# Attention over a K/V cache with two MLP branches: reading K, V and the left-over weight rows in longer elements that feed several partitions

## The chip, the cores and the metric

One core of a Trainium2 chip. The metric is the device time of one execution in microseconds; 214.95 us is the median of three runs of the kernel before (214.92 to 214.96). Engines: PE does matmuls (PEld loads their weights), DVE, ACT and POOL do elementwise work, SP issues nearly all transfers. Sixteen DMA engines move the data.

## The reference

Four sequences (B = 4) with one new token of width 576 each. `out = x + A(LN(x)) + M(LN(x))`.

- A is attention: `q = LN(x) @ wq` gives 32 heads of 128; the cache holds 16 K and V heads, each used by two q heads, of which the last 2,048 positions count; then softmax, the product with V and `@ wo`.
- M normalizes again, goes through `w1` and a gelu, shifts four quarters of the columns along the sequence (with one token all of them become zero), `@ w2`, adds; then a layer norm, `w3` to width 4,608, gelu, `w4`, adds.

Nearly everything that is read is read once: K and V are 16 heads x 2 MB each (67.1 MB), the weights 21.4 MB.

## The kernel before

All is bf16 in memory. A unit of work is one K or V head *g* for all four sequences: 4 x 2,048 positions x 128, a tile of [128 partitions x 8,192 elements], 2 MB. The 2,048 positions are cut into 32 pieces *i* of 64 consecutive positions, and partition `4 i + b` holds piece *i* of sequence *b*: 16,384 B in a row (`kv_pairs`, L231). The K ring has four slots and the V ring four (`NKS`, `NVS`).

Weights of 576 rows are laid out as 4 x 128 rows ("main", four consecutive rows a partition) and 64 left-over rows ("rag"). A left-over row is halved over two partitions, so these 64 rows also fill 128 partitions (`rag_src`, L183). Such rests exist for wq, w1, w2 and w3, of 4,096, 576, 576 and 4,608 B a partition.

Every instruction is put in a list for its engine with a key, and the lists are sorted by key (L563), so the order of the work is fixed by hand. `add_dma` (L172) puts a transfer in SP's list; each transfer has 16 counts on its semaphore. SP issues in this order: wq, w1, w2, w3; the K tiles 0 to 8, V tile 0, K tiles 9 to 15; V tiles 1 to 3; wo into K slots; V tiles 4 to 15; w4 in five pieces. From K tile 4 on, SP waits for PE to be through with the tile four before (`T..`); V likewise (`PV..`); wo waits for K tile 14.

PE's work, in the same order:

- the front: transposes of the normalized x, q (L301), the two small products of M, and w3 (L515);
- K: each tile is transposed in 64 matmuls (L337) with `perm_k` as the moving operand. `perm_k` is a permutation that also sorts the columns from `(i b)` to `(b i)`, so that sequence *b* finds its positions side by side (`kttile`, L76). DVE and ACT copy the results out of PSUM (L344, L345); the scores are 16 matmuls a tile (L353);
- the softmax: exponentials by ACT (L384), 32 x 32 transposes by DVE (L387) and a matmul with `perm_p` (L388), which puts the probabilities on the partitions that V has. `bmask` (L407) marks which sequence a partition belongs to;
- V: 64 matmuls a tile (L434), then wo (L449, L464), w4 (L449, L531), two copies and the output from two queues (L558).

`perm_k` and `perm_p` are made by POOL (L207, L209) and `bmask` by DVE (L407), all from one identity matrix at the start.

Of the kernel before, what the change touches and what calls it, by code (L numbers as in the profile page):

```python
# [8 lines left out]
ALU = mybir.AluOpType  # L9
AX = mybir.AxisListType  # L10


NKS = 4
NVS = 4
# [24 lines left out]
def bass_parallel_sum__sliding_block_cached__mixer_s_mlp__decode_kernel(  # L39
    nc, A_x, A_k_cache, A_v_cache, A_wq, A_wo, B_x, B_w1, B_w2, B_w3, B_w4, out  # L40
):
    B, Sq, D = A_x.shape
    _, Hkv, Sk, Dh = A_k_cache.shape
    Hq = A_wq.shape[1] // Dh
    F = B_w3.shape[1]
    W = min(4096, max(256, Sk // 4))
    assert (B, D, Hkv, Dh, Hq, W, Hq // Hkv, F) == (4, 576, 16, 128, 32, 2048, 2, 4608)
    G = Hkv
    NT = W // 32
    UE = NT * 128  # L50
# [11 lines left out]
    with ExitStack() as ctx:  # L62
# [7 lines left out]
        vring_t = sb("vring", [128, NVS * UE], BF16)  # L70
# [7 lines left out]
        w3rag = regB_t[:, 4 * F:W3E]  # L78
        wqmain = vring_t[:, 0:4 * Hq * Dh].rearrange("p (r n) -> p r n", r=4)
        wqrag = vring_t[:, 4 * Hq * Dh:4 * Hq * Dh + Hq * Dh // 2]  # L80
        wo_sb = kring_t[:, 0:32 * D].rearrange("p (r n) -> p r n", r=32)
        _o = 4 * Hq * Dh + Hq * Dh // 2
        w1main = vring_t[:, _o:_o + 4 * D].rearrange("p (r n) -> p r n", r=4)
        _o += 4 * D
        w1rag = vring_t[:, _o:_o + HALF]
        _o += HALF
        w2main = vring_t[:, _o:_o + 4 * D].rearrange("p (r n) -> p r n", r=4)
        _o += 4 * D
        w2rag = vring_t[:, _o:_o + HALF]
# [22 lines left out]
        ident_bf = sb("ident_bf", [128, 128], BF16)  # L112
        perm_k = sb("perm_k", [128, 128], BF16)
        perm_p = sb("perm_p", [128, 128], BF16)
        bmask = sb("bmask", [128, B, 2], FP32)
# [42 lines left out]
        S = {}  # L158
# [9 lines left out]
        def add(engine, emit, waits=(), sig=None, key=0.0, loop=None):  # L168
            seqc[0] += 1
            prog[engine].append(Op(emit, waits, sig, key, seqc[0], loop))  # L170

        def add_dma(pairs, skey, waits=(), key=0.0, engine="sp"):  # L172
            if skey not in S:
                S[skey] = sem("s_" + "_".join(str(k) for k in (skey if isinstance(skey, tuple) else (skey,))))
            dma_count[skey] = dma_count.get(skey, 0) + 16 * len(pairs)

            def emit(e):
                for o_, i_ in pairs:
                    e.dma_start(o_, i_).then_inc(S[skey], 16)  # L179
            add(engine, emit, waits, None, key)  # L180
            return ("dma", skey, dma_count[skey])

        def rag_src(w_ap):  # L183
            return w_ap[512:576, :].rearrange("r (h n) -> (r h) n", h=2)

        KS = float(NHB + 4)
        KV = KS + 4.0
# [3 lines left out]
        P = lambda *a, **k: add("pool", *a, **k)  # L191
# [10 lines left out]
        def first_counts(e):  # L202
# [1 line left out]
                e.sem_inc(S[("eb", 32 - NTB + k)], 1)  # L204
                e.sem_inc(S[("on", k)], 1)
        P(first_counts, key=-95.7)
        P(lambda e: e.tensor_copy(out=perm_k[:].rearrange("p (b i) -> p b i", b=B), in_=ident_bf[:].rearrange("p (i b) -> p b i", b=B)),  # L207
          waits=["ident_bf"], sig="perm_k", key=-95.5)
        P(lambda e: e.tensor_copy(out=perm_p[:].rearrange("p (i b) -> p i b", b=B), in_=ident_bf[:].rearrange("p (b i) -> p i b", b=B)),  # L209
          waits=["ident_bf"], sig="perm_p", key=-95)  # L210
        P(lambda e: e.memset(ident_f[:], 1.0), sig="if1", key=-94)
        P(lambda e: e.affine_select(out=ident_f[:], in_=ident_f[:], compare_op=ALU.is_equal, fill=0.0, base=0,
# [6 lines left out]
        ev_wq, ev_w3, ev_k, ev_v, ev_w4 = [], [], [], [], []  # L219
        wq_src = A_wq[0:512, :].rearrange("(p r) n -> p r n", r=4)  # L220
        for r in (0, 2):
            ev_wq += 2 * [add_dma([(wqmain[:, r:r + 2, :], wq_src[:, r:r + 2, :])], ("wq", r), (), -20 + r)]
        ev_wq.append(add_dma([(wqrag, rag_src(A_wq))], ("wq", 4), (), -15))
        ev_w1 = add_dma([(w1main, B_w1[0:512, :].rearrange("(p r) n -> p r n", r=4)), (w1rag, rag_src(B_w1))], "w1", (), -14)
        ev_w2 = add_dma([(w2main, B_w2[0:512, :].rearrange("(p r) n -> p r n", r=4)), (w2rag, rag_src(B_w2))], "w2", (), -13)
        w3_src = B_w3[0:512, :].rearrange("(p r) n -> p r n", r=4)
        for r in (0, 2):
            ev_w3 += 2 * [add_dma([(w3main[:, r:r + 2, :], w3_src[:, r:r + 2, :])], ("w3", r), (), -12 + r)]
        ev_w3.append(add_dma([(w3rag, rag_src(B_w3))], ("w3", 4), (), -8))

        def kv_pairs(ring_t, slot, cache, g):  # L231
            return [(ring_t[:, slot * UE:(slot + 1) * UE],
                     cache[:, g, Sk - W:Sk, :].rearrange("b (i t) d -> i b (t d)", t=NT))]

        for g in range(G):
            ev_k.append(add_dma(kv_pairs(kring_t, g % NKS, A_k_cache, g), ("k", g % NKS),
                                [f"T{8 * (g - NKS) + 7}"] if g >= NKS else [], g))
        wo_wait = f"T{8 * (G - 2) + 7}"
        for g in range(G):
            kk = KS + g if g else V0_AFTER + 0.5  # L240
            w = [f"PV{g - NVS}"] if g >= NVS else (["hs1"] if g < WQ_SLOTS else [])
            ev_v.append(add_dma(kv_pairs(vring_t, g % NVS, A_v_cache, g), ("v", g % NVS), w, kk))
            if g == WO_AFTER:
                ev_wo = add_dma([(kring_t[:, 0:32 * D], A_wo.rearrange("(p r) n -> p (r n)", r=32))],
                                "wo", [wo_wait], kk + 0.1)
# [113 lines left out]
        for n in range(NHB):  # L359
            p = n % 32  # L360
# [3 lines left out]
            eng, f = evac(n)  # L364
# [32 lines left out]
        for g in range(G):  # L397
# [6 lines left out]
        add("dve", lambda e: e.reciprocal(out=rinv[:], in_=rsum[:]), waits=["rsum"], sig="rinv", key=KS + 0.36)  # L404
        add("dve", lambda e: e.tensor_scalar(out=diag[:], in0=ident_f[:], scalar1=rinv[:, 0:1], scalar2=None, op0=ALU.mult),
            waits=["rinv", "ident_f"], sig="diag", key=KS + 0.37)
        add("dve", lambda e: e.tensor_reduce(out=bmask[:, :, 0], in_=ident_bf[:].rearrange("p (i b) -> p b i", b=B), axis=AX.X, op=ALU.add),  # L407
            waits=["ident_bf"], sig="bmask0", key=-41)
        add("dve", lambda e: e.tensor_copy(out=bmask[:, :, 1], in_=bmask[:, :, 0]), waits=["bmask0"], sig="bmask", key=-40.9)
        add("pe", lambda e: e.matmul(rinvps, lhsT=ones_f[:], rhs=diag[:], start=True, stop=True), waits=["diag", "ones_f", "PTs3"],  # L410
# [235 lines left out]
```

## Time and profile before

| | us |
|---|---|
| median of three runs | 214.95 |
| the profiled execution | 215.35 |
| its span, from the first to the last instruction | 214.0 |
| packets of SP's queue | 6,920, 88.50 MB |
| HBM read over the span | 414 GB/s |

The profile is of one execution, so sums over its rows are made against 215.35 and its span. "PE 139.3 (65%)" means that matmuls ran in 139.3 us of the span. In the rows of forty slices each digit is a tenth of busy time in 5.35 us. The chain of waits is followed back from the last instruction, at each step to what released it. In the rows on DMA issues the last column is the median time from issue to landing, which includes the wait behind earlier transfers. The share of a queue is the time that its packets took, of 16 engines; over a short window it can come out over 100%, since a packet is counted whole where it starts.

### The profile page before, as it was taken

To read this page: it belongs to the slowest core of one execution; us is meant where nothing else is said; L and a number is where in the kernel's file an instruction comes from. 1 tells how busy PE (TensorE), PEld (TensorE's weight loads), DVE (VectorE), ACT (ScalarE), POOL (GpSimd) and SP (SyncE) were. 2 spreads that over 40 slices of the span, in tenths; PEclk is the share of its full clock that TensorE was granted. 3 is DMA by queue.
4 is the path that set the end of the run, shared out by engine and by line. 5 is a ranking of instruction groups with operands and counts; after the bars stand their busy time and mean duration, and the time that the engine had idled before them with its cause. 6 is when DMAs were issued, how large, how long until landed. Compare 5 with 4: busy or idle time off the path is not lost.

```text
span 214.0 us, 5789 instructions
## 1 busy us (share of the span) xinstructions
PE 139.3 (65%) x2670; PEld 108.2 (51%) x2672; DVE 85.1 (40%) x162; ACT 59.3 (28%) x72; POOL 10.8 (5%) x38
## 2 busy tenths in 40 slices
PE   0368375999999994999999719913344443333585
PEld 0114222877777883788887604813333443333444
DVE  5502602666666664466666569611111111100000
ACT  2001222466665553265666653000000000000000
POOL 8201000000000000000000000000000000000000
PEclk9999855899999999699999995555555555555579
DMA  7999999999999999999999999999999999999992
GB/s 243 426 398 447 441 405 435 416 424 426 432 423 429 429 432 426 429 429 430 426 429 429 432 429 441 423 423 426 426 432 429 423 429 426 429 432 425 428 408 108
DMA packets 6946, 88.63 MB, mean 414 GB/s; under 512 B 781, under 2 KB 1177, under 8 KB 1945
## 3 DMA queue, kind: packets, MB, share of 16 engines
q1 hardware_dynamic: 6920, 88.50, 97.7%
q8 instruction: 7, 0.11, 0.2%
q14 instruction: 3, 0.02, 0.0%
q10 hardware_dynamic: 16, 0.01, 0.0%
HBM read 88.49 MB, written 0.00 MB: 414 GB/s over the span
## 4 chain that ended last, share of the span: by engine, by line
DMA 52%; PE 36%; DVE 4%; SPq 4%; issue 2%; ACT 0%
DMA vring<-in_A_v_cache_dram 23%; PE ps L337 23%; DMA kring<-in_A_k_cache_dram 21%; DMA vring<-in_B_w_dram 8%; PE ps L353 7%; PE ps L434 4%; SPq L179 4%; PE ps L531 1%; DVE PTb L387 1%; DVE rmax L379 1%; DVE regB L345 1%; DVE PTs L395 1%; PE ps L410 0%; ACT P_sb L384 0%; DVE out_sb L558 0%
## 5 line engine op out<-in xcount | busy, mean ns | idle before, releaser
L345 DVE COPY regB<-ps 128x1024 bf16<-128x1024 bf16 x80 | 52.4, 687 | 34.3 <-PE ps L337 32.5
L337 PEld LDWEIGHTS ps<-perm_k,kring 128*128 128x128 bf16 x1024 | 58.9, 99 | 11.9 <-issue 8.6
L337 PE MATMUL ps<-perm_k,kring 128*128 128x128 bf16 x1024 | 62.2, 222 | 3.5 <-DMA kring<-in_A_k_cache_dram 3.5
L344 ACT ACTIVATE regB<-ps 128x1024 bf16<-128x1024 bf16 x48 | 47.6, 1022 | 41.1 <-PE ps L337 41.1
L434 PE MATMUL ps<-PTg,vring 128*128 128x8 bf16 x1024 | 29.5, 168 | 39.4 <-DMA vring<-in_A_v_cache_dram 37.0
L434 PEld LDWEIGHTS ps<-PTg,vring 128*128 128x128 bf16 x1024 | 28.4, 104 | 40.4 <-DMA vring<-in_A_v_cache_dram 27.5
L442 DVE TENSOR_TENSOR PTb<-ps,PTb 128x32 bf16<-128x32 f32 x16 | 3.1, 191 | 56.5 <-PE ps L434 56.5
L353 PE MATMUL ps<-regB,Qs 128*32 128x512 bf16 x272 | 18.8, 397 | 4.6 <-issue 3.5
L541 ACT ACTIVATE P_sb<-ps 100x288 f32<-100x288 f32 x1 | 0.4, 410 | 75.8 <-PE ps L449 75.8
L353 PEld LDWEIGHTS ps<-regB,Qs 128*32 128x32 bf16 x272 | 6.6, 97 | 10.8 <-issue 6.4
L398 DVE TENSOR_TENSOR PTg<-PTs,bmask 128x512 bf16<-128x512 bf16 x16 | 10.7, 681 | 0.0
L375 POOL COPY Qs<-Qpad 128x128 bf16<-128x128 bf16 x16 | 4.6, 293 | 92.6 <-PE ps L353 81.2
L515 PE MATMUL ps<-regB,x1nT 128*32 128x432 bf16 (+1 forms) x60 | 5.4, 520 | 1.9 <-DMA regB<-in_B_w_dram 1.4
L279 PE MATMUL ps<-ident_bf,xn_bf 4*128 4x4 bf16 x8 | 0.6, 170 | 8.8 <-DVE ragsrc L272 8.8
L301 PE MATMUL ps<-vring,xnT 128*32 128x512 bf16 x40 | 4.6, 629 | 2.1 <-DMA vring<-in_A_wq_dram 2.1
L388 PE MATMUL ps<-PTb,perm_p 128*128 128x512 bf16 x3 | 1.8, 609 | 4.9 <-DVE PTb L387 4.8
L279 PEld LDWEIGHTS ps<-ident_bf,xn_bf 4*128 4x128 bf16 x8 | 0.4, 112 | 8.8 <-POOL ones_f L215 6.3
L528 DVE STREAM_TRANSPOSE h2T_sb<-PTb 128x1152 bf16<-128x1152 bf16 x1 | 1.4, 1378 | 8.3 <-ACT PTb L525 8.3
L515 PEld LDWEIGHTS ps<-regB,x1nT 128*32 128x32 bf16 x60 | 2.0, 132 | 4.8 <-DMA regB<-in_B_w_dram 2.7
L558 DVE CAST out_sb<-ps 36x144 bf16<-36x144 f32 x1 | 0.3, 300 | 9.8 <-PE ps L531 9.8
L449 PE MATMUL ps<-kring,ORT 128*4 128x288 bf16 x64 | 3.8, 429 | 0.4 <-DVE ORT L463 0.4
L265 ACT ACTIVATE sd<-mv 4x1 f32<-4x1 f32 x3 | 0.6, 202 | 12.1 <-DVE mv L263 12.1
(98 smaller groups left out, 72.0 us busy)
## 6 DMA issues: line engine op xcount, KB each, us to landing
kring<-in_A_k_cache_dram SPq DMA_DIRECT2D x16, 2048.0 KB, 15.7
vring<-in_A_v_cache_dram SPq DMA_DIRECT2D x16, 2048.0 KB, 17.6
regB<-in_B_w_dram SPq DMA_DIRECT2D x2, 2304.0 KB, 21.5
kring<-in_A_wo_dram SPq DMA_DIRECT2D x1, 4608.0 KB, 24.0
vring<-in_A_wq_dram SPq DMA_DIRECT2D x2, 2048.0 KB, 9.8
vring<-in_B_w_dram SPq DMA_DIRECT2D x2, 2016.0 KB, 17.5
vring<-in_B_w_dram SPq DMA_DIRECT2D x2, 576.0 KB, 13.8
vring<-in_B_w_dram SPq DMA_DIRECT2D x1, 720.0 KB, 14.3
```

Of the source, the lines that this page charges most:

```text
L179: e.dma_start(o_, i_).then_inc(S[skey], 16)
L301: ins = e.matmul(Qps[32 * j:32 * j + 32, k, :], lhsT=x_, rhs=w, start=(r == 0), stop=(r == 4), tile_position=(0, 32 * j))
L337: ins = e.transpose(tb[n % NTB][:, t, :], kring[:, g % NKS, 8 * k + t, :], perm_k[:])
L344: return "act", lambda e: e.activation(out=ktbuf[:, n % NKT], in_=src, func=ACTF.Copy)
L345: return "dve", lambda e: e.tensor_copy(out=ktbuf[:, n % NKT], in_=src)
L353: ins = e.matmul(Sps[32 * b:32 * b + 32, c4, :].rearrange("p (t i) -> p t i", t=16), lhsT=Qs[:, g % 4, b, :], rhs=kttile[:, t0:t0 + 16, b, :],
L375: P(lambda e, g=g: e.tensor_copy(out=Qs[:, g % 4], in_=Qpad[:, g]), waits=(["qT"] if g == 0 else []) + ([f"SC{g - 4}"] if g >= 3 else []), ...
L398: add("dve", lambda e, g=g: e.tensor_tensor(out=PTg[:, g % NPG], in0=PTs[:, :, 2 * g:2 * g + 2].unsqueeze(2).to_broadcast([128, NT, B, 2]) ...
L434: ins = e.matmul(OTps(g), lhsT=vring[:, g % NVS, t, :], rhs=PTg[:, g % NPG, t].rearrange("p b e -> p (b e)"), start=(t == 0), stop=(t == N ...
L442: add("dve", lambda e, g=g: e.tensor_tensor(out=OTx[:, :, 2 * g:2 * g + 2, :], in0=OTps(g).rearrange("p (b e) -> p b e", b=B).unsqueeze(3) ...
L449: return e.matmul(ACC[h], lhsT=lhsT, rhs=rhs, start=start, stop=stop, tile_position=(k0, 32 * h))
L515: ins = e.matmul(H2ps[k][32 * j:32 * j + 32, :], lhsT=x_, rhs=w, start=(r == 0), stop=(r == 4), tile_position=(0, 32 * j))
```

## The change

K and V: the 2,048 positions are cut into 16 pieces *i* of 128 consecutive positions, 32,768 B each. The source of a transfer has 16 x 4 such elements, the destination has 128 partitions of 16,384 B as before: an element of the source fills two partitions, so that position half *j* of piece *i* of sequence *b* is on partition `8 i + 2 b + j`. A new helper, `copy_folded`, builds this copy directly on SP's queue, since the two sides no longer have elements of one length. `perm_k`, `perm_p` and `bmask` follow the new order.

Left-over rows: the source is now 16 elements of four whole rows each, which fill eight partitions; the partition of each half row stays as it was.

The names and the sizes of the tiles, the semaphores, the waits and the order of all lists stay.

```diff
--- before.py
+++ after.py
@@ -169,19 +169,23 @@
             seqc[0] += 1
             prog[engine].append(Op(emit, waits, sig, key, seqc[0], loop))
 
-        def add_dma(pairs, skey, waits=(), key=0.0, engine="sp"):
+        def copy_folded(e, dst, src):
+            return e.add_instruction(mybir.InstDMACopy(mode="Copy", name=f"I-{nc.next_id()}", engine=e.engine, ins=e.lower_ap_dma(src),
+                                                       outs=e.lower_ap_dma(dst), queue="qSPDynamicHW"))
+
+        def add_dma(pairs, skey, waits=(), key=0.0, engine="sp", folded=()):
             if skey not in S:
                 S[skey] = sem("s_" + "_".join(str(k) for k in (skey if isinstance(skey, tuple) else (skey,))))
             dma_count[skey] = dma_count.get(skey, 0) + 16 * len(pairs)
 
             def emit(e):
-                for o_, i_ in pairs:
-                    e.dma_start(o_, i_).then_inc(S[skey], 16)
+                for n, (o_, i_) in enumerate(pairs):
+                    (copy_folded(e, o_, i_) if n in folded else e.dma_start(o_, i_)).then_inc(S[skey], 16)
             add(engine, emit, waits, None, key)
             return ("dma", skey, dma_count[skey])
 
         def rag_src(w_ap):
-            return w_ap[512:576, :].rearrange("r (h n) -> (r h) n", h=2)
+            return w_ap[512:576, :].rearrange("(e r) n -> e (r n)", e=16)
 
         KS = float(NHB + 4)
         KV = KS + 4.0
@@ -204,9 +208,9 @@
                 e.sem_inc(S[("eb", 32 - NTB + k)], 1)
                 e.sem_inc(S[("on", k)], 1)
         P(first_counts, key=-95.7)
-        P(lambda e: e.tensor_copy(out=perm_k[:].rearrange("p (b i) -> p b i", b=B), in_=ident_bf[:].rearrange("p (i b) -> p b i", b=B)),
+        P(lambda e: e.tensor_copy(out=perm_k[:].rearrange("p (b i j) -> p b i j", b=B, j=2), in_=ident_bf[:].rearrange("p (i b j) -> p b i j", b=B, j=2)),
           waits=["ident_bf"], sig="perm_k", key=-95.5)
-        P(lambda e: e.tensor_copy(out=perm_p[:].rearrange("p (i b) -> p i b", b=B), in_=ident_bf[:].rearrange("p (b i) -> p i b", b=B)),
+        P(lambda e: e.tensor_copy(out=perm_p[:].rearrange("p (i b j) -> p i b j", b=B, j=2), in_=ident_bf[:].rearrange("p (b i j) -> p i b j", b=B, j=2)),
           waits=["ident_bf"], sig="perm_p", key=-95)
         P(lambda e: e.memset(ident_f[:], 1.0), sig="if1", key=-94)
         P(lambda e: e.affine_select(out=ident_f[:], in_=ident_f[:], compare_op=ALU.is_equal, fill=0.0, base=0,
@@ -220,26 +224,26 @@
         wq_src = A_wq[0:512, :].rearrange("(p r) n -> p r n", r=4)
         for r in (0, 2):
             ev_wq += 2 * [add_dma([(wqmain[:, r:r + 2, :], wq_src[:, r:r + 2, :])], ("wq", r), (), -20 + r)]
-        ev_wq.append(add_dma([(wqrag, rag_src(A_wq))], ("wq", 4), (), -15))
-        ev_w1 = add_dma([(w1main, B_w1[0:512, :].rearrange("(p r) n -> p r n", r=4)), (w1rag, rag_src(B_w1))], "w1", (), -14)
-        ev_w2 = add_dma([(w2main, B_w2[0:512, :].rearrange("(p r) n -> p r n", r=4)), (w2rag, rag_src(B_w2))], "w2", (), -13)
+        ev_wq.append(add_dma([(wqrag, rag_src(A_wq))], ("wq", 4), (), -15, folded=(0,)))
+        ev_w1 = add_dma([(w1main, B_w1[0:512, :].rearrange("(p r) n -> p r n", r=4)), (w1rag, rag_src(B_w1))], "w1", (), -14, folded=(1,))
+        ev_w2 = add_dma([(w2main, B_w2[0:512, :].rearrange("(p r) n -> p r n", r=4)), (w2rag, rag_src(B_w2))], "w2", (), -13, folded=(1,))
         w3_src = B_w3[0:512, :].rearrange("(p r) n -> p r n", r=4)
         for r in (0, 2):
             ev_w3 += 2 * [add_dma([(w3main[:, r:r + 2, :], w3_src[:, r:r + 2, :])], ("w3", r), (), -12 + r)]
-        ev_w3.append(add_dma([(w3rag, rag_src(B_w3))], ("w3", 4), (), -8))
+        ev_w3.append(add_dma([(w3rag, rag_src(B_w3))], ("w3", 4), (), -8, folded=(0,)))
 
         def kv_pairs(ring_t, slot, cache, g):
-            return [(ring_t[:, slot * UE:(slot + 1) * UE],
-                     cache[:, g, Sk - W:Sk, :].rearrange("b (i t) d -> i b (t d)", t=NT))]
+            return [(ring_t[:, slot * UE:(slot + 1) * UE].unsqueeze(1),
+                     cache[:, g, Sk - W:Sk, :].rearrange("b (i t) d -> i b (t d)", t=2 * NT))]
 
         for g in range(G):
             ev_k.append(add_dma(kv_pairs(kring_t, g % NKS, A_k_cache, g), ("k", g % NKS),
-                                [f"T{8 * (g - NKS) + 7}"] if g >= NKS else [], g))
+                                [f"T{8 * (g - NKS) + 7}"] if g >= NKS else [], g, folded=(0,)))
         wo_wait = f"T{8 * (G - 2) + 7}"
         for g in range(G):
             kk = KS + g if g else V0_AFTER + 0.5
             w = [f"PV{g - NVS}"] if g >= NVS else (["hs1"] if g < WQ_SLOTS else [])
-            ev_v.append(add_dma(kv_pairs(vring_t, g % NVS, A_v_cache, g), ("v", g % NVS), w, kk))
+            ev_v.append(add_dma(kv_pairs(vring_t, g % NVS, A_v_cache, g), ("v", g % NVS), w, kk, folded=(0,)))
             if g == WO_AFTER:
                 ev_wo = add_dma([(kring_t[:, 0:32 * D], A_wo.rearrange("(p r) n -> p (r n)", r=32))],
                                 "wo", [wo_wait], kk + 0.1)
@@ -404,7 +408,7 @@
         add("dve", lambda e: e.reciprocal(out=rinv[:], in_=rsum[:]), waits=["rsum"], sig="rinv", key=KS + 0.36)
         add("dve", lambda e: e.tensor_scalar(out=diag[:], in0=ident_f[:], scalar1=rinv[:, 0:1], scalar2=None, op0=ALU.mult),
             waits=["rinv", "ident_f"], sig="diag", key=KS + 0.37)
-        add("dve", lambda e: e.tensor_reduce(out=bmask[:, :, 0], in_=ident_bf[:].rearrange("p (i b) -> p b i", b=B), axis=AX.X, op=ALU.add),
+        add("dve", lambda e: e.tensor_reduce(out=bmask[:, :, 0], in_=ident_bf[:].rearrange("p (i b j) -> p b i j", b=B, j=2), axis=AX.XY, op=ALU.add),
             waits=["ident_bf"], sig="bmask0", key=-41)
         add("dve", lambda e: e.tensor_copy(out=bmask[:, :, 1], in_=bmask[:, :, 0]), waits=["bmask0"], sig="bmask", key=-40.9)
         add("pe", lambda e: e.matmul(rinvps, lhsT=ones_f[:], rhs=diag[:], start=True, stop=True), waits=["diag", "ones_f", "PTs3"],
```

## The prediction

> **What bounds the kernel now.** The page's first lines come first: the busy shares, then the row of DMA load by slices, then the queues.
>
> ```profile
> span 214.0 us, 5789 instructions
> PE 139.3 (65%) x2670; PEld 108.2 (51%) x2672; DVE 85.1 (40%) x162; ACT 59.3 (28%) x72; POOL 10.8 (5%) x38
> ...
> DMA  7999999999999999999999999999999999999992
> GB/s 243 426 398 447 441 405 435 416 424 426 432 423 429 429 432 426 429 429 430 426 429 429 432 429 441 423 423 426 426 432 429 423 429 426 429 432 425 428 408 108
> ...
> q1 hardware_dynamic: 6920, 88.50, 97.7%
> ```
>
> No compute engine is over 65% busy. The 16 DMA engines are at 9 in every slice but the first and the last, and the packets of SP's queue (q1) take 97.7% of 16 x 214.0 us: 209.1 us of full load on each engine. The other 4.9 us of the span are the start before data flows and the end after the last byte. In the chain of waits, pieces in order of time, two stretches matter.
>
> ```profile
> 36.41 1.89 PE ps L337 x16
> ...
> 39.45 3.71 PE ps L337 x64
> 43.15 0.24 issue
> 43.40 1.05 PE ps L353 x16
> ...
> 150.42 1.88 PE ps L434 x64
> ...
> 152.32 17.64 DMA vring<-in_A_v_cache_dram
> ...
> 170.01 1.88 PE ps L434 x64
> ...
> 189.60 1.88 PE ps L434 x64
> ...
> 209.03 3.11 PE ps L531 x88
> ...
> 212.17 0.30 DVE out_sb L558
> ```
>
> The columns are start, duration and what was waited for. In the V stage PE does a tile in 1.88 us and then waits; its turns come four tiles apart, 170.01 - 150.42 = 19.59 us, and again 189.60 - 170.01 = 19.59 us, so 4.90 us a tile of 2 MB. That is the pace of the DMA engines. In the K stage the chain runs along PE, 3.71 + 0.24 + 1.05 = 5.00 us a tile, while the GB/s row stays level: the transfers do not wait for PE there, because they run tiles ahead. I therefore count the time in DMA load. PE's K stage is a cover that has to be examined below.
>
> How that load divides between bytes and packets is read from the DMA view over short windows. It takes the packets that start in a window; their summed time is the share times 16 engines times the window. First 79.84 to 79.85 us, with two packets that only count a semaphore up (each transfer ends with one on each engine):
>
> ```profile
> q1 hardware_dynamic: 2, 0.00, 11.2%
> ```
>
> 0.112 x 0.16 us / 2 = **9.0 ns** each, with next to no data. Then 15.21 to 15.22 us, left-over rows of w1, 576 B a packet:
>
> ```profile
> q1 hardware_dynamic: 9, 0.01, 163.1%
> ```
>
> 1.631 x 0.16 us / 9 = 29.0 ns. 12.5 to 13.6 us, left-over rows of wq, 4,096 B a packet, seven semaphore packets among them:
>
> ```profile
> DMA packets 118, 0.45 MB, mean 413 GB/s; under 512 B 7, under 2 KB 7, under 8 KB 118
> ...
> q1 hardware_dynamic: 118, 0.45, 100.6%
> ```
>
> (1.006 x 17.6 us - 7 x 0.009) / 111 = 159 ns. 146 to 200 us, V, 16,384 B a packet:
>
> ```profile
> DMA packets 1589, 23.13 MB, mean 428 GB/s; under 512 B 176, under 2 KB 176, under 8 KB 176
> ...
> q1 hardware_dynamic: 1588, 23.12, 100.6%
> ```
>
> (1.006 x 864 us - 176 x 0.009) / 1,412 = 614.4 ns. Last 129 to 137 us, wo, 36,864 B a packet:
>
> ```profile
> DMA packets 94, 3.47 MB, mean 433 GB/s; under 512 B 0, under 2 KB 0, under 8 KB 0
> ...
> q1 hardware_dynamic: 94, 3.47, 100.5%
> ```
>
> 1.005 x 128 us / 94 = 1,368.5 ns.
>
> From V to wo 20,480 B more take 754 ns, 0.0368 ns a byte. That leaves 614.4 - 603.3 = 11 ns of each V packet that its bytes do not explain; of the 4,096-byte packet 159 - 150.8 = 8 ns; of the 576-byte packet 29.0 - 21.2 = 8 ns. The shares are rounded to 0.1%, which moves the first by about 1 ns, the others by less. So a packet costs 8 to 12 ns beside its bytes, and a packet with no data 9.0 ns. I take **9 ns**.
>
> **The change part by part.**
>
> *K and V.* A tile is 128 runs of 16,384 B, eight on each engine. Now the source is 16 x 4 runs of 32,768 B, four on each engine, and each run fills two neighbouring partitions. The order of partitions is chosen so that the two halves of a run, which follow each other in memory, stand next to each other; the bytes are the same. If a packet is one read run, each engine has 8 - 4 = 4 packets less a tile, so 4 x 9 = 36 ns of its 4.90 us. Over the 32 tiles:
>
> ```profile
> kring<-in_A_k_cache_dram SPq DMA_DIRECT2D x16, 2048.0 KB, 15.7
> vring<-in_A_v_cache_dram SPq DMA_DIRECT2D x16, 2048.0 KB, 17.6
> ...
> kring<-in_A_wo_dram SPq DMA_DIRECT2D x1, 4608.0 KB, 24.0
> ...
> regB<-in_B_w_dram SPq DMA_DIRECT2D x1, 576.0 KB, 26.1
> vring<-in_A_wq_dram SPq DMA_DIRECT2D x1, 512.0 KB, 12.8
> ...
> vring<-in_B_w_dram SPq DMA_DIRECT2D x2, 72.0 KB, 13.7
> ```
>
> 32 x 4 = 128 packets less on each engine, 128 x 9 ns = **1.15 us**.
>
> *Left-over rows.* Four transfers (wq 512 KB, w1 and w2 72 KB each, w3 576 KB) go from eight reads on each engine to one that feeds eight partitions: 4 x 7 = 28 packets less, 28 x 9 ns = **0.25 us**. The partition of each half row is the old one.
>
> *Bigger reads by themselves.* Reads of 32,768 and 36,864 B are no new size: wo's 36,864-byte packets run at 433 GB/s against 428 GB/s for V. What no row shows is a read whose length is not that of its write; every transfer of before has both alike. The saving is therefore bounded as follows. If the overhead belongs to the write runs, of which there are as many as before, it is 0. If it belongs to the reads, it is 156 x 8 to 12 ns, 1.25 to 1.87 us. If dividing a read between partitions costs time of its own, it is negative; that is the third rival. I take the reads at 9 ns, nearest to the semaphore packet, which has its fixed cost whatever it moves: 156 x 9 ns = **1.40 us**.
>
> [...]
>
> *The permutations.* perm_k, perm_p and bmask are built once by strided copies and a reduction, now with one more dimension.
>
> ```profile
> 1.87 0.29 DVE L407 TENSOR_REDUCE bmask<-ident_bf 128x4 f32<-128x128 bf16 x1 [1.87 <-POOL ident_bf L194]
> ...
> 4.80 0.28 POOL L207 COPY perm_k<-ident_bf 128x128 bf16<-128x128 bf16 x1
> ...
> 5.03 0.38 POOL L209 COPY perm_p<-ident_bf 128x128 bf16<-128x128 bf16 x1
> ...
> 9.35 1.04 PE L301 MATMUL ps<-vring,xnT 128*32 128x512 bf16 x8
> ```
>
> They take 0.29, 0.28 and 0.38 us and the same elements; even at double length they end before 7 us, and PE's first work on a transferred weight starts at 9.35. perm_k is first used on K at 36.41 us. Cost 0, hidden by the transfer of wq. Without that cover it would be at most the 0.95 us that they take now. PE, ACT and the matmuls keep their shapes.
>
> *Waits and queues.* No wait is added or moved; SP issues the same transfers in the same order. What shifts is how close the slots' release comes to an empty queue. The tight place is the change from K to V, in the rows of SP's own instructions:
>
> ```profile
> 116.73 0.33 SPq L179 DMA_DIRECT2D kring<-in_A_wo_dram  x1
> 134.31 3.95 SPq L179 DMA_DIRECT2D vring<-in_A_v_cache_dram  x3
> ```
>
> wo is the last transfer ahead of V's fifth tile. It lands 24.0 us after 116.73, at 140.7; the tile is issued at 134.31, once PE has used the first V tile, 6.4 us earlier. With the change wo lands sooner by 20 tiles x 36 ns + 0.25 = 0.97 us. PE, bound by its 5.00 us a tile, moves at least by what K's first tile gains, 0.25 + 0.04 = 0.29 us. The cover shrinks to some 5.7 us and stays. Should it go, each microsecond of a late issue costs one, since all 16 engines would stand idle. In the K stage PE now lags by 5.00 - 4.86 = 0.14 us a tile, over 16 tiles 2.2 us, against a ring of four tiles; in the V stage PE needs 1.88 us of 4.86. Nothing else becomes late: after the last byte the same 3.11 us of matmuls, copies and the output remain.
>
> *Sum.* 209.1 - 1.15 - 0.25 = 207.7 us of load, span 212.6 us. The profiled execution took 215.35 us, 1.35 more than its span, and becomes 213.95; the median of the runs lies 0.40 under it at 214.95, so the median becomes **213.55 us**, 0.65% faster.
>
> **The rivals.**
>
> 1. *No change: the write runs set the price.* The packets that the trace lists could be those of the writes, and each engine still writes eight runs of 16,384 B a tile; or the reads are cut to the shorter side again, so that the change does not do what it says. For it: before has no unlike pair that would tell. Against: nothing in the rows prefers the write side. 214.95 us.
> 2. *Half the price.* Read and write each carry half of the 9 ns: 156 x 4.5 = 0.70 us, 214.25 us. [...] Against: the smallest data packet already has its 8 ns whole.
> 3. *Slower: the seam between two partitions costs time.* Packets now follow one another without a gap (their times fill 100.5 to 100.7% of the engines, so they even overlap a little). If an engine has to change the write address in the middle of a packet, it may stop for it. There are as many seams as packets saved: one in each of 128 reads, seven in each of four, 156. Up to 9 ns a seam the change still gains; from there it loses. Priced like the shortest data packet, 29 ns, it is 156 x (29 - 9) = 3.1 us: 218.05 us. For it: no row shows such a read. Against: engines already go from one write run to the next eight times a tile within the 8 to 12 ns. A stop that waits for the write to land would cost far more, beyond what I think likely.
>
> **How the numbers follow.** Forecast (reads carry the price, 8 to 12 ns) 0.62; half the price 0.08; no change 0.13; seams that cost more than they save 0.17. The forecast's own range is 213.0 (12 ns: 214.95 - 1.87 = 213.08, and scatter) to 213.8 us. The range that I give reaches down to 212.9 and up past the two middle cases to 215.1, 0.15 over the median for scatter; it leaves out the seams, 0.17. A measurement of this kernel can tell about 0.2%, 0.43 us, from no change: faster 0.62 + 0.08 = 0.70, same 0.13, slower 0.17.
>
> **What would show it.** In the profile after: packets of SP's queue fall by 156 x 16 = 2,496 to about 4,420 and their mean is a little over twice the time of 16 KB in V's windows, near 1,217 ns; PE's turns four V tiles apart come 19.45 us apart, not 19.59; the queue's load falls by 1.4 us and the span with it. If the packets still number 6,920 and the turns stay at 19.59, it is rival 1; turns of 19.52 are rival 2; turns over 19.59, with DMA still at 9 throughout, rival 3. The forecast's frame is wrong if DMA falls under 9 between 120 and 145 us (the cover from K to V was too small) or if PE starts to wait at other places than K and V tiles.

## The result and the profile after

| | before | after |
|---|---|---|
| median of six runs | 214.95 us | 368.93 us |
| the profiled execution | 215.35 us | 368.35 us |
| its span | 214.0 us | 367.1 us |
| packets of SP's queue | 6,920 | 4,424 |

The changed kernel takes 1.712 times as long (95% interval 1.709 to 1.715); two of its six runs, at 374 us, count as slow and are not in the ratio. The forecast was 213.55 us.

The page of after, the lines that answer to the first ones shown of before:

```profile
span 367.1 us, 5791 instructions
...
PE 157.3 (43%) x2672; PEld 117.1 (32%) x2672; DVE 85.3 (23%) x162; ACT 60.8 (17%) x72; POOL 10.7 (3%) x38
...
DMA  8999999999999999999999998999999999999995
GB/s 315 367 420 285 196 229 224 227 221 214 211 218 225 225 221 211 214 219 229 225 221 229 223 229 320 319 229 225 221 229 211 221 207 229 221 225 225 203 353 224
...
q1 hardware_dynamic: 4424, 88.50, 98.6%
```

The DMA row looks as it did: all 16 engines are busy from end to end. The GB/s row does not. The first three slices (wq, w1, w2, w3), the two of wo (320 and 319) and the one of w4 (353) move 315 to 420 GB/s, and all slices with K or V alone sit at 196 to 229, about half of the 405 to 441 of before. The engines are as busy as before and deliver half: under K and V a 9 in the DMA row stood beside 405 to 441 GB/s before and stands beside 196 to 229 here, so the two rows have to be read together.

PE's granted clock was lower too, 0.693 on average against 0.777, and its matmuls took 157.3 us in place of 139.3. That is not the loss: in the K and V stages PE waits for data, and the same transfers are as slow in a kernel without PE work (214 GB/s in group b of e1 below).

The chain of waits of after, V stage (start, duration, what was waited for):

```profile
257.04 1.88 PE ps L438 x64
258.92 0.02 issue
258.93 36.16 DMA vring<-in_A_v_cache_dram
...
295.14 1.88 PE ps L438 x64
...
333.27 1.88 PE ps L438 x64
```

PE's turns, four tiles apart, come 295.14 - 257.04 = 38.10 us apart (38.13 the next time) where they came 19.59 apart: 9.53 us a tile, not 4.90. The DMA view of after from 258 to 296 us:

```profile
DMA packets 317, 8.29 MB, mean 218 GB/s; under 512 B 64, under 2 KB 64, under 8 KB 64
...
q1 hardware_dynamic: 317, 8.29, 99.5%
```

317 packets less 64 that count semaphores are 253 reads of 32,768 B; 0.995 x 608 us / 253 is 2.39 us each, less a few hundredths for the 64. Two reads of 16,384 B took 1.23 us. So the packets are the reads, as forecast, and each takes twice as long as its bytes did.

Sum: 32 tiles x (9.53 - 4.90) = 148 us of the 153.0 us between the profiled executions. The folded left-over rows are 2.6 us more (e3 below). Some 2 us are left, among them plain transfers that follow a folded one: wo's 128 packets took 1.51 us on average where they took 1.37 before, so eight of them 12.1 us in place of 10.9.

### The profile page after: what moved, and what is told of

Same layout as the page of the kernel before. It is cut to its first block, busy times and chain, and to the rows that moved or that the text cites. A ratio compares the mean times of both kernels' runs of the same rounds, so it can differ in the third digit from the quotient of the medians.

```text
span 367.1 us, 5791 instructions
## 1 busy us (share of the span) xinstructions
PE 157.3 (43%) x2672; PEld 117.1 (32%) x2672; DVE 85.3 (23%) x162; ACT 60.8 (17%) x72; POOL 10.7 (3%) x38
## 3 DMA queue, kind: packets, MB, share of 16 engines
q1 hardware_dynamic: 4424, 88.50, 98.6%
## 4 chain that ended last, share of the span: by engine, by line
DMA 80%; PE 13%; DVE 2%; another core or an unknown queue 2%; SPq 2%; issue 1%; ACT 0%
DMA kring<-in_A_k_cache_dram 42%; DMA vring<-in_A_v_cache_dram 31%; DMA vring<-in_B_w_dram 7%; PE ps L341 7%; PE ps L438 2%; PE ps L357 2%; PE ps L535 1%; SPq L183 1%; DVE PTb L391 1%; SPq L173 1%; DVE rmax L383 1%; DVE regB L349 0%; DVE PTs L399 0%; PE ps L414 0%
## 5 line engine op out<-in xcount | busy, mean ns | idle before, releaser
L341 PE MATMUL ps<-perm_k,kring 128*128 128x128 bf16 x1024 | 74.1, 240 | 67.0 <-DMA kring<-in_A_k_cache_dram 67.0
L341 PEld LDWEIGHTS ps<-perm_k,kring 128*128 128x128 bf16 x1024 | 67.9, 109 | 80.9 <-DMA kring<-in_A_k_cache_dram 52.4
L438 PE MATMUL ps<-PTg,vring 128*128 128x8 bf16 x1024 | 29.5, 168 | 112.8 <-DMA vring<-in_A_v_cache_dram 112.8
L348 ACT ACTIVATE regB<-ps 128x1024 bf16<-128x1024 bf16 x48 | 49.1, 1023 | 117.1 <-PE ps L341 117.1
L357 PE MATMUL ps<-regB,Qs 128*32 128x512 bf16 x272 | 25.3, 509 | 1.2 <-DVE regB L349 1.2
L535 PE MATMUL ps<-vring,h2T_sb 128*4 128x144 bf16 x88 | 3.1, 226 | 0.6 <-DMA vring<-in_B_w_dram 0.6
L388 ACT ACTIVATE P_sb<-ps,negb 128x512 bf16<-128x512 f32 x4 | 2.7, 685 | 2.4 <-DVE negb L384 2.4
```

The costliest lines, as they stand in the source:

```text
L341: ins = e.transpose(tb[n % NTB][:, t, :], kring[:, g % NKS, 8 * k + t, :], perm_k[:])
L348: return "act", lambda e: e.activation(out=ktbuf[:, n % NKT], in_=src, func=ACTF.Copy)
L357: ins = e.matmul(Sps[32 * b:32 * b + 32, c4, :].rearrange("p (t i) -> p t i", t=16), lhsT=Qs[:, g % 4, b, :], rhs=kttile[:, t0:t0 + 16, b, :],
L438: ins = e.matmul(OTps(g), lhsT=vring[:, g % NVS, t, :], rhs=PTg[:, g % NPG, t].rearrange("p b e -> p (b e)"), start=(t == 0), stop=(t == N ...
L535: return e.matmul(FIN[h][z], lhsT=lhsT, rhs=rhs, start=start, stop=stop, tile_position=(0, 32 * h))
```

## The experiments

The trace of after already speaks against the prediction's rival with seams (changes of partition inside a read). The folded left-over row of wq, 32,768 B with seven changes of partition, took 1.76 to 2.14 us a packet in the trace, less than K's 2.39 us with one. So the loss is not a fixed price for each seam.

Three theories were set against each other. **A**: what costs is which partitions the engines write at the same time; 16 pieces of eight neighbouring partitions make engines collide that did not before. **B**: a read that feeds several partitions runs at half pace. **C**: reads of 32,768 B in this order are slow at the source.

### e1: the transfers alone

A kernel that only moves data, in groups that are waited for; it computes nothing and writes zeros. The forms of the copy (K's cache as source, `flat` is one stretch of memory):

```diff
+def as_after(g):
+    return folded(slot(g % 4).unsqueeze(1), win(g).rearrange("b (i t) d -> i b (t d)", t=128))
+def flat_grouped(n, groups):      # 32 or 16, one read per partition
+    return folded(slot(n).unsqueeze(1), flat(n, 128, UE).rearrange("(i k) x -> i k x", i=groups))
+def flat_folded(n, rows, length): # 64, 32 or 16 reads of 32,768 B
+    return folded(ring[:, n * w:(n + 1) * w], flat(n, rows, length))
+def half_folded(n, p0):           # two sequences into 64 partitions from p0
+    ...                           # src: two sequences of K's window, 16 x 2 reads
+    return folded(slot(n % 4, p0, p0 + 64).unsqueeze(1), src)
```

> The transfers alone: no attention, no MLP, output zeros. Eleven groups one after the other: a (K as before, 8 MB), b (K as after, 8 MB), c (plain rows of 32,768 B, 8 MB), d and e (plain, 16,384 B on both sides, one stretch of memory, its source written as 32 x 4 or 16 x 8 rows, 8 MB each), f, g, h (folded: 64, 32, 16 reads of 32,768 B feeding 2, 4, 8 partitions, 8, 4, 2 MB), i, j, k (folded as b, two sequences, partitions 0-63, 32-95, 64-127, 4 MB each). a should take 20 us (4.90 us a tile), b 38 us (9.53 us in the V stage of after). Theory A: an engine feeds several partitions at full pace; slow is the set of partitions that the 16 engines write at the same time, from 16 pieces of eight neighbours. Then e is as slow as b though it folds nothing (38 us), c and d fast (20), f and g fast if their pieces are dealt as before's 32 are (20 and 10), h slow (10), and of i, j, k, alike but for the partitions, some fast (10) and some slow (19). [...] Theory B: changing the partition inside a read halves an engine's pace: c, d, e fast; f, g, h, i, j, k slow (38, 19, 10; 19 each). Theory C: reads of 32,768 B are slow: c, f, g, h, i, j, k slow, e fast.

Each window below reaches from one transfer's first semaphore count to a later one's, so it holds whole transfers. Group b (as after), d (plain, 32 x 4), e (plain, 16 x 8), f (folded, 64 reads):

```profile
DMA packets 240, 6.29 MB, mean 214 GB/s; under 512 B 48, under 2 KB 48, under 8 KB 48
...
DMA packets 433, 6.29 MB, mean 431 GB/s; under 512 B 49, under 2 KB 49, under 8 KB 49
...
DMA packets 432, 6.29 MB, mean 215 GB/s; under 512 B 48, under 2 KB 48, under 8 KB 48
...
DMA packets 239, 6.29 MB, mean 432 GB/s; under 512 B 47, under 2 KB 47, under 8 KB 47
```

The first two numbers tell how the bytes came: about 190 reads of 32,768 B or about 384 of 16,384 B for the same 6.29 MB. The third is the pace. d and e read the same stretch into the same partitions in plain reads and differ only in how the copy groups them: 431 against 215 GB/s. f folds every read over two partitions and runs at 432. So B is out, and so is C (f reads 32,768 B; plain reads of that length, group c, also ran at full pace, 426 GB/s from 68 to 84 us, and 208 of them took (0.986 x 256 us - 0.14) / 208 = 1.213 us each). Groups i and j, folded, from the same source into partitions 0-63 and 32-95:

```profile
DMA packets 143, 3.15 MB, mean 206 GB/s; under 512 B 47, under 2 KB 47, under 8 KB 47
...
DMA packets 145, 3.15 MB, mean 429 GB/s; under 512 B 49, under 2 KB 49, under 8 KB 49
```

Nothing differs but the partitions, and the pace doubles. Since source and reads are the same, the memory that is read from is out as a cause too. k (64-127) is slow like i (208 GB/s). g was fast, (1.054 x 112 us - 0.4) / 96 = 1.23 us a read from 178 to 185 us; h (16 reads feeding eight partitions) was slow, (0.91 x 80 us - 0.3) / 33 = 2.20 us a read from 190 to 195 us. In every group it is theory A that says which are slow and which fast.

### e2 and e3: the two halves of the change alone

e2 leaves out the four folds of the left-over rows, e3 leaves K, V and the permutations as before:

```diff
 # e2
-            return w_ap[512:576, :].rearrange("(e r) n -> e (r n)", e=16)
+            return w_ap[512:576, :].rearrange("r (h n) -> (r h) n", h=2)
 # e3
-                     cache[:, g, Sk - W:Sk, :].rearrange("b (i t) d -> i b (t d)", t=2 * NT))]
+                     cache[:, g, Sk - W:Sk, :].rearrange("b (i t) d -> i b (t d)", t=NT))]
```

> The left-over rows are read as before, only K and V are folded. All theories: the 32 tiles are the loss, 32 x (9.53 - 4.90) = 148 us; the folded rows' own share is the rest. Some 366 us (365 to 368), against 368.35 us for the profiled run of after.

Measured 372.07 us, one run, above the 365 to 368 expected. After's own six runs lie from 367.1 to 374.3 us, so the few microseconds of the left-over rows can't be read from it; K and V are practically the whole loss.

> K and V as before, only the four left-over transfers folded, seven changes of partition inside each read. In the trace of after K's first tile landed some 2 us later than its own loss explains. If a folded read runs at about half pace (theories A and B), 1.2 MB take 2.8 us more at most: 216.5 to 217.8 us. If each change of partition cost a fixed 1.16 us (what one costs in K's reads: 2,385 ns a packet, where 16,384 B twice take 1,229), the four transfers would cost 28 x 1.16 = 32 us: 247 us.

Measured 217.59 us, ratio 1.0118 (1.0101 to 1.0135): within what half pace gives, 2.6 us. The 32 us of a fixed price of 1.16 us a seam did not come.

### e4: other partitions, and other folds of the left-over rows

> The transfers alone, output zeros. a, b, c, d: the folded form of K for two sequences (4 MB, every engine four neighbouring partitions) into the 64 partitions from 16, 32, 48 and 64. After e1 theory A stands (from 32: 10.6 us, from 0 or 64: about 20 us). Its sharper form: an engine and the engine four further share a way into the memory wherever both write groups of four partitions whose numbers differ by 32 below or above partition 64. From 32 no two engines collide, from 64 all do; from 16 and from 48 eight engines collide with one other and eight with none. So b is as fast as in e1 (10.6 us, all packets near 1,215 ns), d about 20 us (near 2,520), and a and c have both kinds of packet, half of them near 1,215 and half near 2,400 to 2,520 ns, about 20 us long. If only a border at partition 64 mattered, a and c would hold one kind, between. e, f, g, h: the left-over rows of wq eight times (4 MB), as 128 plain reads of 4,096 B, and as 64, 32 and 16 reads that feed 2, 4 and 8 partitions. Theory A: h at half pace (19 us), f and g at full pace and shorter than e by 9 ns a packet saved: per engine 64, 32, 16 packets, so f 0.29 us and g 0.43 us under e (about 10.2 us and a start).

The DMA view of groups a, b and c (from partition 16, 32, 48):

```profile
DMA packets 143, 3.15 MB, mean 214 GB/s; under 512 B 47, under 2 KB 47, under 8 KB 47
...
DMA packets 143, 3.15 MB, mean 432 GB/s; under 512 B 47, under 2 KB 47, under 8 KB 47
...
DMA packets 143, 3.15 MB, mean 207 GB/s; under 512 B 47, under 2 KB 47, under 8 KB 47
```

b came as expected (432 GB/s), and so did d: (0.98 x 208 us - 0.3) / 80 = 2.54 us a read from 65 to 78 us. a and c did not: the 96 reads in each window took 2.46 us on average in a and 2.54 in c ((1.007 x 16 x 14.71 us - 0.4) / 96 and (1.005 x 16 x 15.22 - 0.4) / 96), where half of them at 1.22 would have left the mean near 1.83. So not half of them but practically all were slow. The sharper form of A was wrong in this, or incomplete. The left-over rows: transfers of 512 KB followed each other at 1.25 us each as 128 plain reads, at 1.23 to 1.28 us as 64 or 32 reads, and at 2.14 us as 16. That is near half pace for the form of the change. The other two show no gain clear of their scatter, where 0.29 and 0.43 us over eight transfers were expected.

### e5 and e6: folding without collisions in the kernel

e5 is e3 with 32 reads that feed four partitions; e6 also brings wq's and w3's main parts in one transfer each (wq shown):

```diff
-            return w_ap[512:576, :].rearrange("(e r) n -> e (r n)", e=16)
+            return w_ap[512:576, :].rearrange("(e r) n -> e (r n)", e=32)
 # e6
-        for r in (0, 2):
-            ev_wq += 2 * [add_dma([(wqmain[:, r:r + 2, :], wq_src[:, r:r + 2, :])], ("wq", r), (), -20 + r)]
+        ev_wq += 4 * [add_dma([(wqmain, wq_src)], ("wq", 0), (), -20)]
```

> The kernel before with the four left-over transfers folded into 32 reads, each feeding four partitions, in place of 16 feeding eight. Theory A: full pace, and two packets in place of eight on each engine: 4 x 6 x 9 ns = 0.22 us less, 214.75 us (ratio 0.9990). Theory B, which e1 has against it: half pace as in e3, 217.6 us. If the fixed cost belonged to the write runs: 214.97 us.

> As e5, and the main parts of wq and w3, which came in two transfers each of 16,384 and 18,432 B a partition, come in one each: plain reads of 32,768 and 36,864 B. That is 8 packets less on each engine for each, and one semaphore packet less: 2 x (8 x 9 + 9) = 0.16 us on top of e5: 214.6 us (ratio 0.9982). Against it: PE's q and w3 stages start later, but K's first tile, which PE needs next, lands at 36 us.

e5: 215.06 us, ratio 1.0003 (0.9994 to 1.0012). The loss of e3 is gone, and the expected 0.9990 lies outside the interval. e6: 214.92 us, 0.9994 (0.9979 to 1.0009); its expectation of 0.9982 and no change both lie inside. 384 and 672 packets fewer brought nothing that shows.

### e7: two, four and eight engines

e4's open point, with reads from one stretch and fewer engines:

```diff
+def dealt(n, engines, rows, p0):
+    ...                           # src: rows / 2 reads of 32,768 B from one stretch
+    src = src.rearrange("(i k t) d -> i k (t d)", i=engines, t=128)
+    return folded(slot(n % 4, p0, p0 + rows).unsqueeze(1), src)
```

> The transfers alone, output zeros. Reads of 32,768 B from one stretch, each feeding two partitions; what changes is how many engines take part and which partitions each writes. e4 left open why from partition 16 and 48 all engines were slow. P (sharing): two engines on one way into the memory take twice as long (some 2,450 ns a packet), an engine alone on its way does not (1,215 ns). Q (coupling): where any two collide all engines slow down. R (own way): an engine is fast only into the groups of four partitions that a plain transfer gives it, whether others collide or not. a (16 engines, from 32): all fast, 2.43 us a transfer of 1 MB. b and c (16 engines, from 36 and from 40): 2 and 4 of 16 engines collide: P has 1/8 and 1/4 of the packets slow, Q and R all. d, e, f (8 engines, 32 partitions from 0, 64, 16: no two collide): P and Q all fast, 2.43 us a transfer of 512 KB; R has d fast, e and f slow (4.9 us). g, h (2 engines, 32 partitions each, from 0 and from 32): by P and Q g is slow (38 us for 1 MB: engine one writes 0-31, the other 32-63) and h fast (19.4 us); by R both slow. i (4 engines, from 32, none collide): 9.7 us by P and Q. j (4 engines, from 16; two collide, two do not): P half the packets slow, Q all.

Groups g (98 to 115 us) and h (137 to 152 us), two engines into partitions 0-63 and into 32-95, as the copy groups them one on 0-31 and the other on 32-63, then on 32-63 and 64-95; the share is of 16 engines, so 12.5% is two engines busy:

```profile
q1 hardware_dynamic: 15, 0.49, 12.5%
...
q1 hardware_dynamic: 25, 0.82, 12.6%
```

0.125 x 16 x 17 us / 15 = 2.27 us a packet in g, 0.126 x 16 x 15 / 25 = 1.21 us in h. Two engines are enough: with 14 engines idle, two that fill partitions 0-63 take nearly twice as long for a read as two that fill 32-95. d, e and f, eight engines into 32 partitions from 0, 64 and 16, where by the theories no two collide, all ran at full pace (R is out): (0.487 x 80 us - 0.1) / 32 = 1.21 us a read in d from 62 to 67 us, (0.508 x 96 us - 0.2) / 40 = 1.21 in e and in f, from 74 to 80 and from 87 to 93 us. Group b, where by the theories two of 16 collide, from 18 to 24 us and from 26 to 34 us:

```profile
DMA packets 116, 2.39 MB, mean 399 GB/s; under 512 B 43, under 2 KB 43, under 8 KB 43
...
q1 hardware_dynamic: 116, 2.39, 98.3%
...
DMA packets 9, 0.20 MB, mean 25 GB/s; under 512 B 3, under 2 KB 3, under 8 KB 3
...
q1 hardware_dynamic: 9, 0.20, 11.4%
```

The six reads of the second window took 0.114 x 128 us / 6 = 2.43 us each. The 73 of the first took (0.983 x 96 us - 0.4) / 73 = 1.29 us on average, which is what 14 engines at 1.21 us and two at 2.43 give: 14 go through, and two are left behind and finish alone. That is P. In j, from 172 to 180 us, 18 reads took 0.221 x 128 us / 18 = 1.57 us on average, near the 1.62 that two engines at 1.21 us and two at 2.43 give, also P. But in c, where by the theories four of 16 collide, 80 reads from 42 to 55 us took (0.981 x 208 us - 0.3) / 80 = 2.55 us on average, as in a and c of e4, which looks like Q. Why all engines slow down there stays open.

### e8, e9, e10: the whole kernel with other deals

Each tile is read from one stretch of memory (not the data that the reference wants), since only then can the copy's source be written as 128, 64 or 16 x 8 equal steps. e9 and e10 use `copy_folded`; the lines on the source:

```diff
-                     cache[:, g, Sk - W:Sk, :].rearrange("b (i t) d -> i b (t d)", t=NT))]
+                     cache[0, g].rearrange("(p t) d -> p (t d)", t=NT))]                       # e8
+                     cache[0, g].rearrange("(p t) d -> p (t d)", t=2 * NT))]                   # e9
+                     cache[0, g].rearrange("(i k t) d -> i k (t d)", i=16, t=NT))]             # e10
```

> The kernel before, but each tile is read from one stretch of 2 MB (all 8,192 positions of the first sequence's head) as 128 plain reads of 16,384 B: other data than the reference wants, the same bytes and the same work. It is the yardstick for the next two. If the place of the source matters little, 215.0 us; all theories agree.

> As e8, but each tile is 64 reads of 32,768 B, each feeding two partitions: as many reads and as long as in after, and as many changes of partition inside them, dealt to the engines in 64 pieces of two partitions in place of 16 pieces of eight (other data than the reference wants, the same work). Theory A (what costs is two engines writing the same way into the memory; a read that feeds two partitions costs nothing): no loss, and a gain of 32 x 20 ns = 0.64 us by e1's pace of the same transfers alone (4.84 against 4.86 us a tile), or 1.15 us by the 9 ns a packet of the prediction: 214.4 or 213.9 us if e8 takes 215.0. Theory B (a change of partition inside a read costs): some 365 us.

> As e8, plain reads of 16,384 B that feed one partition each, nothing folded, but the copy's source is written as 16 groups of eight reads, so that each engine gets eight neighbouring partitions as in after (other data than the reference wants, the same work). Theory A: as slow as after without its folded left-over rows, 365 to 372 us (e1: 9.76 us a tile). Theory B and theory C (length of the reads): 215 us.

e8: 215.03 us, 0.9999 (0.9990 to 1.0008). e10: 370.98 us, one run, with plain reads of 16,384 B and not one folded read. Its page:

```profile
GB/s 312 436 417 262 211 215 216 209 218 211 222 218 209 223 220 209 220 215 214 218 214 220 220 218 369 296 213 218 216 218 218 214 220 213 213 218 214 220 367 214
...
q1 hardware_dynamic: 6920, 88.50, 98.8%
```

The packets number 6,920 as before and the pace is that of after: the loss comes without one longer or folded read. e9, with after's 64 reads of 32,768 B that feed two partitions each, took 215.02 us, 0.9998 (0.9989 to 1.0007). So the loss is gone, and the gain is not there. Turns of PE in the V stage, e8 and then e9:

```profile
169.77 1.88 PE ps L438 x64
...
189.35 1.88 PE ps L438 x64
```

```profile
169.75 1.89 PE ps L438 x64
...
189.33 1.88 PE ps L438 x64
```

19.58 us for four tiles in both, where the prediction's 9 ns would have made it 0.14 us less and e1's pace 0.08. The DMA view from 40 to 120 us, e8 and then e9:

```profile
DMA packets 2344, 34.18 MB, mean 427 GB/s; under 512 B 257, under 2 KB 257, under 8 KB 257
...
q1 hardware_dynamic: 2340, 34.13, 100.3%
```

```profile
DMA packets 1304, 34.23 MB, mean 428 GB/s; under 512 B 257, under 2 KB 257, under 8 KB 257
...
q1 hardware_dynamic: 1300, 34.18, 100.2%
```

Less the 257 semaphore packets at 9 ns, e8 has (1.003 x 1,280 - 2.3) us / 2,083 = 615 ns for 16,384 B and e9 (1.002 x 1,280 - 2.3) / 1,043 = 1,227 ns for 32,768 B. Two short packets are 1,230 ns: the long one saves 3 ns, not 9, and that doesn't shorten the turns.

## Why the prediction was wrong

- *What bounds the kernel now*: right. Each engine's load is the time, before and after (97.7% and 98.6% of the spans); PE's cover never came into play.
- *K and V*, the step that failed: "The order of partitions is chosen so that the two halves of a run, which follow each other in memory, stand next to each other; the bytes are the same." The bytes are; the deal is not. Source steps of 32 x 4 became 16 x 4, and with them, by the inference below, the set of partitions that the engines write at one time. No step of the prediction asked which engine writes where, although the order of the partitions was part of the change. e1's d against e, and e10 against e8, show that another grouping of the source alone, without one longer read, halves the pace of the transfers (215 in place of 431 GB/s; 370.98 in place of 215.03 us). The size is 148 us where the step had -1.15 us.
- *Left-over rows*: the same failure, +2.6 us in place of -0.25 us (e3); with 32 pieces it is gone (e5, 215.06 us).
- *Bigger reads by themselves*, the price of 9 ns a packet: wrong as well, and a second step that failed. As a record it holds: in e1 plain packets of 16,384 B (group d) took 611 ns and of 32,768 B (group c) 1,213, 9 less than two short ones. But the records overlap a little (shares of 100.5 to 100.7%), and what overlaps is not time. From landing to landing a tile alone took 4.84 us in f and 4.86 in d by the author's reading, some 5 ns for each packet saved; the windows whose rows stand above, 14.57 us for three tiles of f and 14.59 of d, give 2. In the kernel not even that came: e9 has 2,048 packets fewer and ends where e8 does (215.02 and 215.03 us). So with a deal like e9's the forecast would have been wrong too, and "no change" (rival 1) right in its time, though not in its reason, since the packets are the reads. Why the kernel shows none of it is open; e9's reads took 1,227 ns there, 14 more than c's. (In the reading of V, 73 of the 1,412 packets are pieces of w4, of 16,128 B; without them, at 605 ns each, the 11 ns would be 12.)
- The mark "packets fall to about 4,420" was met, 4,424. It showed that the reads were joined, not that this helps.
- *Rival 3* had the sign, and neither mechanism nor size: a read with one seam took 1,217 ns on average in f of e1, a plain one of that length 1,213 in c, and e9 lost nothing (215.02 us). Its mark (turns over 19.59 us with DMA still full) was met all the same; it could not tell seams from anything else that slows the engines. Its price was taken from a short packet; the sentence that a bigger stop is "beyond what I think likely" had no row behind it. The range upwards should have held a halved pace, which needed the question about the deal.
- *The permutations*, *Waits and queues*: nothing speaks against them. PE's waits for V tiles grew from 37.0 to 112.8 us, and the DMA row stayed full.

What is shown and what is argued: that the grouping of the source and the partitions written decide, whatever the reads, is shown (e1: 431 against 215 GB/s for d and e, 429 against 206 for j and i; e10: 370.98 us), and that two engines are enough, 2.27 us a read into partitions 0-63 against 1.21 into 32-95 (e7). Which engine writes which partition no row names; that a copy whose source has 16 outer steps gives each engine eight neighbours is inferred, from d and e, and from b of e7, whose rows fit exactly two engines falling behind. By it, in after engines e and e + 4 write partitions that lie 32 apart, as the two of e7's g would (in e4, with four partitions an engine, e and e + 8). That the pace is 214 to 220 GB/s, half of 431, fits g's reads, which took 1.9 times as long as h's. What two such engines share is not shown; the "way into the memory" of the theories is the author's assumption. Why practically all reads are slow where by it only four or eight engines meet is not explained.

A version that beats both kernels wasn't found. One copy of a K or V tile can't have 32 or 64 even source steps of 32,768 B, since the four sequences lie apart in memory. Several copies a tile, such as e1's j for two sequences, were not tried in the kernel; e9 leaves little hope that they would gain.

## What to carry to other kernels

Here the grouping of a copy's source decided the pace (16 x 8 steps in place of 32 x 4: 215 in place of 431 GB/s in e1), by the author's inference because it sets which partitions are written at once. When a copy is rewritten, compare that before the lengths of the reads, and try the copy alone, one group of a few transfers for each form, before it goes into a kernel. A full DMA row with half the GB/s (196 to 229 in place of 405 to 441) was the sign here of engines in each other's way. Overhead that stands in the records of overlapping packets need not be there to be saved (of 9 ns a packet, e9 with 2,048 packets fewer saved nothing that shows): test it by a pace from landing to landing, and then in the kernel.

## What was not expected of the hardware

- A read of 32,768 B that fills two partitions, or one of 16,384 B that fills four, runs at full pace or near it (432 GB/s in e1's f; 1.23 to 1.28 us for 512 KB in e4, where plain reads took 1.25).
- Two engines that fill partitions 0-63 take 2.27 us on average for 32,768 B, two that fill 32-95 1.21 us (e7's g and h).
- With 16 engines on 64 partitions from 36 the rows fit 14 engines at 1.21 us a read and two at 2.43; from 40, 16 and 48 the mean of all reads is 2.55, 2.46 and 2.54 us (e7's b and c, e4's a and c). Why is open.
- In the kernel a tile takes 4.90 us as 128 reads or as 64 (e8, e9), alone 4.86 and 4.84 (d and f of e1, from landing to landing); reads of 32,768 B take 1,227 ns there, plain ones alone 1,213 (c of e1). What holds the kernel's transfers back by this 1% was not tried.
